# Scales and norms written as rows, weight sums at other periods, one slot without v: attention and feed-forward on one core

## Chip, cores and metric

One core of a Trainium2 chip runs the whole program. The metric is the device time of one execution in microseconds, the median of several executions. TensorE (PE), VectorE (DVE), ScalarE (ACT), GpSimd (POOL) and SyncE (SP) each run their own instructions in order; SP and POOL issue the DMAs here, and a DMA that waits for something holds up what is queued behind it on its issuing engine.

## What is computed

The reference, cut to what matters (B = 4, N = 6080, C = 256, d_ff = 2048, 24320 tokens):

```python
qn = q / (norm(q, axis=1) + 1e-6)
kn = k / (norm(k, axis=1) + 1e-6)
s = kn.transpose(0, 2, 1) @ qn / tau          # C x C scores of each batch
a = exp(s - s.max(-1)); a /= a.sum(-1) + 1e-9
x = (v @ a).reshape(B * N, C)
h = x @ w_in
g = maximum(0.01 * h, h)
out = g @ w_out
```

## The kernel before

The attention matrix of a batch is multiplied into w_in, so that v is taken straight to h; then g and the second product follow. Products are made of f16 or f32 halves: three matmuls each (high by high, low by high, high by low). There are 24 tiles of tokens (6 a batch, 512 or 496 columns twice) and 8 pairs of blocks of d_ff in each; one tile and pair is a **period**, numbered 8 x tile + pair, 192 in all. The first product of a period takes seven block products instead of eight (Strassen's way: sums of blocks are multiplied). From tile 15 to tile 22 (`FAST`, periods 120 to 183) the second product takes seven too, and needs sums of the w_out blocks.

The order of the work is written out when the program is built. Each period has slots on VectorE, ScalarE and TensorE (`slot`, line 1529 and on), each with room for some estimated microseconds. Side work stands in queues and is taken into a slot while it fits; in the slot "dve" the queue "dve_idle" comes last, after everything else. `at(w, fn)` puts work into the queues when period w begins. What an engine runs is in that order.

Buffers called `temp` (nine, `TEMPS`) hold the copies `h` of block products (ScalarE, line 1206, three a period), the output tiles `o_sb`, the squares `sq`, the units of q and k, and the four intermediate tiles of one `wo_sums` job. A buffer is free again when its last reader is through, for an output tile when its store has landed.

The places that the change touches:
- `Scale` (class, line 147 and on) finds one power of two for a tensor: maxima per partition, then the maximum over the partitions. `gather` (line 166) writes the 128 maxima as a column to DRAM from SP (line 170, `v_scale_line` and the like: 128 pieces of 4 bytes), `read` (line 190) a period later reads that line back to all partitions, into the tile `zeros`. It waits on SP until the column has landed. Tiles from 16 on use `spread` (line 174) instead, without DRAM: a copy, a transpose (lines 177, 178) and copies. The way over DRAM is taken twelve times: two weight scales, ten tiles of v.
- `inverse` (line 508) writes the 4 x 128 inverse norms of the last batch as four columns in one DMA from POOL (line 517, `n_line`), and reads them back as a row to all partitions (line 518).
- `wo_sums(m)` (line 1002), m = 0 to 3, makes the w_out sums that the seven products of pairs 2m and 2m + 1 need: two whole-tile additions (line 1012), four half-tile operations (line 1023), and for two results a ScalarE cast (line 1031) and a subtraction (line 1034), all its VectorE steps in "dve_idle". `SUMS_AT` starts jobs 0, 1, 2 at periods 79, 83, 85; job 3 starts behind the last scores product (line 1679).
- `fast_slot` (line 1369) lays out a period of tiles 15 to 22. Its first "dve" slot (line 1388) takes v work, the splitting of the next tile's v into the operands of the first product.
- In the last tile the slot "dve_out" (line 2395) takes additions of line 1327 that finish tile 22's outputs.
- Stores to `w_dram` (line 896, from POOL) write split weights that ScalarE (line 841) and VectorE (line 853) made; their buffers (three, each in two halves) are free when the store has landed.

Of the kernel before, what the change touches and what calls it, by code (L numbers as in the profile page):

```python
# [19 lines left out]
QUAD = 32  # L20
# [10 lines left out]
RBUFS = 4  # L31
RSQRT_MAGIC = float(0x5F3759DF)
TOP = 12
SUMS_AT = (79, 83, 85)
UNITS = 5
SCORES_AT = {1: (8, 20), 2: (48, 22), 3: (0, 0)}
NORMS_AT = 80
# [6 lines left out]
def channel_attention_ffn(  # L44
# [17 lines left out]
    nc = tc.nc  # L62
# [16 lines left out]
    NPAIR = NF // 2  # L79
# [20 lines left out]
    zeros = const.tile([P, P], F32, name="zeros")  # L100
# [3 lines left out]
    ones_r = const.tile([P, P], F32R, name="ones")  # L104
    nc.vector.tensor_scalar(out=ones_r, in0=zeros, scalar1=1.0, scalar2=None, op0=ALU.add)
    ones = ones_r.bitcast(F32)
    exp_bias = const.tile([P, 1], F32, name="exp_bias")
    nc.vector.memset(exp_bias, -896.0 * 2.0**23)
    tau_t = const.tile([P, 1], F32, name="tau_t")
# [37 lines left out]
    class Scale:  # L147
# [18 lines left out]
        def gather(self):  # L166
            last = nc.vector.tensor_reduce(out=self.top, in_=self.most, axis=AX.X, op=ALU.max)
            if self.near:
                return self.spread()
            nc.sync.dma_start(out=self.line, in_=self.top)  # L170
            at(now[0] + 1, self.read)
            return last

# [75 lines left out]
    class Scores:  # L249
# [258 lines left out]
        def inverse(self):  # L508
            t, n = self.nt, 2 * CH
            nc.vector.tensor_tensor(out=t, in0=self.nx, in1=self.ny, op=ALU.mult)  # L510
            nc.vector.tensor_scalar(out=t, in0=t, scalar1=1e-6, scalar2=2.0**-TOP, op0=ALU.add, op1=ALU.mult)
            rn = small.tile([P, n], F32, name="rn")
            last = nc.vector.reciprocal(out=rn, in_=t)
            rows = spare_part(7, 8)
            self.rows = rows.rearrange("p (x c) -> p x c", x=2)
            line = dram.tile([2 * CH, P], F32, name=f"n_line{self.b}")
            nc.gpsimd.dma_start(out=line[0:n, :].rearrange("x p -> p x"), in_=rn[:, 0:n])
            nc.gpsimd.dma_start(out=rows, in_=line[0:n, :].rearrange("x p -> (x p)").partition_broadcast(P))
            at(now[0] + 2, self.start)
            return last  # L520
# [709 lines left out]
    def p_has(g):  # L1230
        return g // NPAIR in FAST
# [137 lines left out]
    def fast_slot(i, p):  # L1369

        g = i * NPAIR + p
        n = widths[i % NT]
        seeded = not (p == 0 and widths[i % NT] > widths[(i - 1) % NT])
        w_split.pop((i, p - 1) if p else (i - 1, NPAIR - 1), None)
        sums_start(g)
        order = ("P5", "P7", "P6", "P1", "P3") if p == 3 else ("P5", "P7", "P1", "P3", "P6")
        fast_outs(g, *order[:4 if p == 4 else 5])
        x, z = bank("x"), bank("z")
        block_product(i, p, x, A11, "B11", True, False)
        if seeded:  # L1380
            run("act", lambda: nc.scalar.copy(out=z[:, 0:n], in_=x[:, 0:n]))
        else:
            h11 = taken(i, x)
        if g - 1 in fast_h:
            run("act", unit, i - (p == 0), (p - 1) % NPAIR, "C12", fast_h.pop(g - 1), True)
        out(6)
        fast_do("act", high, g - 4, "T4")
        slot("dve", 3.0 if not p_has(g - 2) else 1.5)
        block_product(i, p, z, A12, "B21", not seeded, True)
        block_product(i, p, x, S2, "T2", False, False)  # L1390
        if not seeded:
            add(i, h11, z)
        run("act", unit, i, p, "C11", z if seeded else h11)
        h12 = taken(i, x)
        out(4)
        slot("dve_end", 1.5)
        fast_do("act", high, g - 1, "C12")
        run("act", high, i, p, "C11")
        fast_do("act", high, g - 2, "T1")
        fast_do("dve", low, g - 1, "C12")  # L1400
        run("dve", low, i, p, "C11")
        fast_outs(g, "P2", *(["P6"] if p == 4 else []))
        block_product(i, p, z, S1, "T1", True, False)
        block_product(i, p, x, S3, "T3", False, False)
        h22 = taken(i, x)
        add(i, h22, z)
        out(6)
        fast_do("act", high, g - 2, "T3")
        fast_do("act", high, g - 3, "T2")
        slot("act_end", 0.65)  # L1410
        if i == FAST[0]:
            slot("act", 1.4)
        fast_do("dve", low, g - 2, "T1")
        if p == 4:
            slot("dve_end", 0.8)
        fast_do("dve", low, g - 2, "T3")
        if not p_has(g - 2):
            slot("dve", 1.5)
        block_product(i, p, x, A22, "T4", False, True)
        block_product(i, p, z, S4, "B22", False, True)  # L1420
        run("act", unit, i, p, "C21", x, True)
        run("act", unit, i, p, "C22", h22)
        run("act", high, i, p, "C22")
        add(i, h12, z)
        fast_h[g] = h12
        last_outs(g)
        out(15 if p == 3 else 24)
        wide = p in (3, 4) or not p_has(g - 3)
        if not p_has(g - 3):
            run("dve", low, i, p, "C22")  # L1430
        fast_do("dve", low, g - 3, "T2")
        fast_do("dve", low, g - 4, "T4")
        slot("dve_end", 1.5)
        if p_has(g - 3):
            run("dve", low, i, p, "C22")
        if p == 4:
            slot("dve_out", 1.5)
        if p not in (0, 7) or not p_has(g - 3):
            slot("dve", 1.9 if wide else 1.45)
        if i == FAST[0]:  # L1440
            slot("dve_idle", 1.4)
            slot("act", 1.4)
# [215 lines left out]
    def unit_one(sc, j):  # L1658
        unit_ahead.append(j)
        unit_temps.append(j)  # L1660
        t = []
# [8 lines left out]
        def product():  # L1670
            unit_ahead.pop(0)
            unit_go(sc)
            splits.close(sc.at[j])
            if j == 0:
                sc.begin(None, bank("s"))
            mm = sc.product(j)
            if j == NCHUNK - 1:
                norm_work(sc)
                put_steps(wo_sums(NPAIR // 2 - 1), False, True)
            return mm  # L1680

        def low():
# [329 lines left out]
    def put_steps(steps, first, on=True):  # L2012

        def entry(n):
            then = [entry(n + 1)] if n + 1 < len(steps) else ()
            if steps[n][0] == "call":
                return ("call", lambda: (steps[n][1](*steps[n][2:]), *(put(*x) for x in then)))
            return (*steps[n], then, first or n > 0 and on)

        put(*entry(0))  # L2020
# [101 lines left out]
        at(24 + n, lambda n=n: put_steps(wo_half(n), False, False))  # L2122
    for n in range(wo_n):
        at((T16 - 1) * NPAIR + n // 2 * 2 + 3, wo_load, n)
    for m in range(NPAIR // 2 - 1):
        at(SUMS_AT[m], lambda m=m: put_steps(wo_sums(m), False, True))


# [185 lines left out]
    last = None  # L2314
    held = []
    for i in range(NTILES):
        for p in range(NPAIR):
# [15 lines left out]
            x, y, z = bank("x"), bank("z" if i else "y"), bank("z")  # L2333
# [6 lines left out]
            if last is not None:  # L2340
                leaky(i, p - 1, "C12", last)
                last = None
# [47 lines left out]
            else:  # L2390
                last = h12
            out(24)
            if i == NTILES - 1:
                slot("dve_end", 1.5)
                slot("dve_out", 1.5)
            last_outs(now[0])
            if i == NTILES - 1 and p < 4:
                outs.append(ffn_out(i, p, False))
# [37 lines left out]
```

## Time and profile before

| | us |
|---|---|
| median of 3 runs | 2085.36 |
| lowest, highest | 2080.54, 2089.03 |
| the profiled execution | 2087.1 |
| its span, first to last instruction | 2085.3 |
| TensorE busy | 2042.4 |
| VectorE, ScalarE, POOL busy | 1720.5, 1547.6, 340.1 |
| mean granted TensorE clock | 0.995 |

How to read it: all views are of the one profiled execution, in microseconds from its first instruction. PEld is TensorE's weight load, which runs beside its matmuls. A row of the windows view holds a stretch, its length, then the busy time (with the number of instructions) of PE, PEld, DVE, ACT and POOL in it, the granted TensorE clock as a share of full speed, the busy share of the 16 DMA engines and GB/s. In a timeline row the bracket at the end is the idle time of the engine just before and what ended it. A period is taken to begin with its first block product's first matmul: period 58 is 705.3 to 718.9, 89 is 1042.4 to 1066.8, 105 is 1234.1 to 1249.5, 113 is 1325.8 to 1344.0.

### The profile page before, as it was taken

What the parts mean: (1) busy time and instruction counts of PE and PEld (TensorE: products, weight loads), DVE (VectorE), ACT (ScalarE), POOL (GpSimd) and SP (SyncE); (2) the same over time, 40 slices, a digit from 0 to 9 for tenths busy, and PEclk for the clock granted to TensorE, in tenths of its full rate; (3) what the DMA queues carried; (4) which work ended last, traced back from release to release, by engine and by line L of the source; (5) the groups of instructions that cost most, each with busy time, mean ns of one, the idle gap of its engine ahead of it and who ended that gap; (6) DMA issues with size and microseconds to landing.
All of it is one profiled execution on the core that took longest, in us unless ns stands there. A gap on an engine that the chain in (4) does not pass through costs nothing.

```text
span 2085.3 us, 28200 instructions
## 1 busy us (share of the span) xinstructions
PE 2042.4 (98%) x9540; PEld 1185.9 (57%) x9540; DVE 1720.5 (83%) x3143; ACT 1547.6 (74%) x2849; POOL 340.1 (16%) x427
## 2 busy tenths in 40 slices
PE   9999999999999999999979999999999999999999
PEld 8888888888865455544435545444444444444444
DVE  8988888878788788888868878788989888888973
ACT  6577777766578788877756666678988888898874
POOL 0000000000012232120110000004433333343310
PEclk9999999999999999999989999999999999999999
DMA  9945676555576898663543332238998876777630
GB/s 365 395 164 206 202 244 214 178 171 181 184 211 183 226 251 223 188 167 99 162 117 127 107 125 75 102 120 194 198 203 195 176 151 139 141 147 143 134 70 27
DMA packets 158401, 359.84 MB, mean 173 GB/s; under 512 B 19536, under 2 KB 47696, under 8 KB 158256
## 3 DMA queue, kind: packets, MB, share of 16 engines
q1 hardware_dynamic: 104912, 251.52, 36.5%
q0 software_dynamic: 52976, 106.20, 25.8%
q8 instruction: 75, 1.23, 0.2%
q14 instruction: 70, 0.57, 0.1%
q10 hardware_dynamic: 368, 0.32, 0.0%
HBM read 221.77 MB, written 57.42 MB: 134 GB/s over the span
## 4 chain that ended last, share of the span: by engine, by line
PE 85%; DVE 5%; DMA 5%; ACT 3%; issue 1%; POOL 0%; SPq 0%; DVEq 0%; ACTq 0%; POOLq 0%
PE ps_o L1487 30%; PE ps_x L1163 21%; PE ps_z L1163 15%; PE ps_o L1300 7%; PE ps_s L385 4%; PE ps_o L385 2%; PE ps_y L1300 1%; PE ps_s L1300 1%; DVE g_pair L1261 1%; DMA g_a<-g_a 1%; DVE h L1200 1%; PE ps_s L1842 1%; DMA spare<-sq 1%; DMA g_a<-g_b 1%; DMA w_dram<-w_first 1%
## 5 line engine op out<-in xcount | busy, mean ns | idle before, releaser
L1487 PE MATMUL ps_o<-g_split,w_out_split 128*128 128x512 f16 (+3 forms) x2880 | 712.6, 383 | 0.2 <-ACT o_sb L1506 0.2
L1163 PE MATMUL ps_x<-v_split,w_split 128*128 128x512 f16 (+3 forms) x2280 | 621.1, 381 | 26.9 <-ACT h L1206 23.5
L1163 PEld LDWEIGHTS <-w_split 128*128 128x128 f16 x3024 | 293.5, 98 | 385.5 <-issue 54.6
L1200 DVE TENSOR_TENSOR h<-ps_z,h 128x512 f32<-128x512 f32 (+1 forms) x505 | 344.4, 682 | 183.3 <-ACT h L1206 160.5
L1163 PE MATMUL ps_z<-v_split,w_split 128*128 128x512 f16 (+3 forms) x1704 | 462.8, 380 | 9.3 <-DVE h L1200 9.0
L1206 ACT COPY h<-ps_x 128x512 f32<-128x512 f32 (+1 forms) x513 | 295.2, 575 | 190.0 <-PE ps_x L1163 170.2
L1193 DVE TENSOR_TENSOR g_split<-g,g_split 128x512 f16<-128x512 f32 (+3 forms) x480 | 328.6, 685 | 78.4 <-ACT g_split L1183 73.6
L1183 ACT ACTIVATE g<-h 128x512 f32<-128x512 f32 (+1 forms) x384 | 240.0, 625 | 167.9 <-DVE h L1200 165.3
L1487 PEld LDWEIGHTS <-w_out_split 128*128 128x128 f16 x1920 | 188.7, 98 | 226.1 <-issue 5.7
L1487 PEld LDWEIGHTS ps_o<-g_split,w_out_split 128*128 128x128 f32 x1152 | 216.4, 188 | 43.5
L1183 ACT ACTIVATE g_split<-h 128x512 f16<-128x512 f32 (+3 forms) x360 | 220.2, 612 | 0.0
L1261 DVE TENSOR_TENSOR g_pair<-g_b,g_pair 128x512 f16<-128x512 f32 (+1 forms) x192 | 125.1, 679 | 42.0 <-ACT g_pair L1256 41.6
L1300 PE MATMUL ps_o<-g_pair,w_out_split 128*128 128x512 f16 (+1 forms) x576 | 158.0, 377 | 0.4 <-ACT g_pair L1256 0.3
L1300 PEld LDWEIGHTS <-spare 128*128 128x128 f16 x768 | 75.1, 98 | 88.9 <-issue 0.4
L1163 PEld LDWEIGHTS ps_x<-v_split,w_split 128*128 128x128 f32 x576 | 107.8, 188 | 22.3 <-ACT g L1183 0.4
L1256 ACT CAST g_pair<-g_b 128x512 f16<-128x512 f32 (+1 forms) x192 | 111.0, 611 | 0.0
L1109 DVE SCALAR_TENSOR_TENSOR v_split<-v_raw,v_scale,v_split 128x512 f16<-128x512 f32 (+1 forms) x125 | 93.0, 744 | 3.8
L1300 PEld LDWEIGHTS <-w_out_split 128*128 128x128 f16 x576 | 56.3, 98 | 67.0 <-issue 0.6
L273 POOL MEMSET qk_raw<- 64x512 f32 x5 | 3.0, 592 | 538.1 <-ACT sq L299 267.6
L1261 DVE TENSOR_TENSOR g_pair<-g_a,g_pair 128x512 f16<-128x512 f32 (+1 forms) x128 | 86.5, 676 | 1.9 <-ACT g_pair L1256 1.5
L1183 ACT ACTIVATE g<-ps_x 128x512 f32<-128x512 f32 (+1 forms) x128 | 75.3, 588 | 15.5 <-PE ps_x L1163 13.4
L1163 PEld LDWEIGHTS ps_z<-v_split,w_split 128*128 128x128 f32 x408 | 76.2, 188 | 16.6 <-DVE h L1200 1.4
(266 smaller groups left out, 2724.5 us busy)
## 6 DMA issues: line engine op xcount, KB each, us to landing
w_split<-w_dram SPq DMA_DIRECT2D x104, 448.0 KB, 4.0
w_split<-w_dram SPq DMA_DIRECT2D x40, 896.0 KB, 5.1
qk_raw<-in_q_dram SPq DMA_DIRECT2D x115, 256.0 KB, 5.0
qk_raw<-in_k_dram SPq DMA_DIRECT2D x115, 256.0 KB, 5.1
v_raw<-in_vT_dram SPq DMA_DIRECT2D x32, 512.0 KB, 6.0
out_dram<-o_sb SPq DMA_DIRECT2D x64, 256.0 KB, 3.4
spare<-sq POOLq DMA_DIRECT2D x47, 256.0 KB, 6.1
g_a<-g_a POOLq DMA_DIRECT2D x40, 256.0 KB, 3.9
```

The source lines that it names most:

```text
L385: mm = nc.tensor.matmul(out=out, lhsT=lhsT, rhs=rhs, start=start, stop=stop, skip_group_check=True)
L1109: return nc.vector.scalar_tensor_tensor(out=sp[:, 1, 0:w], in0=src, scalar=up, in1=sp[:, 0, 0:w], op0=ALU.mult, op1=ALU.subtract)
L1163: mm = nc.tensor.matmul(out=ps[:, 0:n], lhsT=w[:, x, a, :], rhs=sp[:, y, 0:n], start=first and k == 0, stop=k == 2, skip_group_check=True,)
L1183: return nc.scalar.activation(out=to, in_=h[:, 0:n], func=AF.Prelu, alpha=0.01, scale=G_SCALE if i >= T16 else 1.0)
L1193: issued["dve"] = nc.vector.tensor_tensor(out=sp[:, 1, 0:n], in0=out[:, 0:n], in1=f32(sp[:, 0, 0:n]), op=ALU.subtract)
L1200: issued["dve"] = nc.vector.tensor_tensor(out=h[:, 0:n], in0=ps[:, 0:n], in1=h[:, 0:n], op=ALU.add)
L1206: issued["act"] = nc.scalar.copy(out=h[:, 0:n], in_=ps[:, 0:n])
L1256: return nc.scalar.copy(out=sp[:, 0, 0:n], in_=g32[i, p, HELD.get(name, name)][:, 0:n])
L1261: return nc.vector.tensor_tensor(out=sp[:, 1, 0:n], in0=g32[i, p, HELD.get(name, name)][:, 0:n], in1=sp[:, 0, 0:n], op=ALU.subtract)
L1300: issued["pe"] = nc.tensor.matmul(out=ps[:, 0:n], lhsT=fast_lhsT(i, p, prod, x), rhs=sp[:, y, 0:n], start=p == 0 and k == 0, stop=p == NPA ...
L1487: issued["pe"] = nc.tensor.matmul(out=o_ps[i][j][h][:, 0:n], lhsT=wo_lhsT(i, x, f, h), rhs=sp[:, y, 0:n], start=p == 0 and early and k == ...
L1842: last = nc.tensor.matmul(out=ps, lhsT=m[:, x, W_OF[n] * P:(W_OF[n] + 1) * P], rhs=r[:, y, :], start=n in W_OPENS and k == 0, stop=k == 2, ...
```

## The change

Scales and norms go to DRAM as rows: a new helper `turned` copies the columns into 32 columns of `zeros`, transposes 32 by 32 blocks on VectorE, and gives one view of 4 partitions x 32 for each column; line 170's DMA then has 4 pieces of 128 bytes, and line 517's DMA becomes four such DMAs. `SUMS_AT` becomes 79, 113, 121, 122 and starts all four jobs; the start of job 3 behind the last scores product goes. The first "dve" slot of a seven-product period has room 0 in pair 4, where it had 1.5, once such periods are under way. The last tile's "dve_out" slot has room for 0.8 us instead of 1.5. The arithmetic is the same.

```diff
--- before.py
+++ after.py
@@ -31,7 +31,7 @@
 RBUFS = 4
 RSQRT_MAGIC = float(0x5F3759DF)
 TOP = 12
-SUMS_AT = (79, 83, 85)
+SUMS_AT = (79, 113, 121, 122)
 UNITS = 5
 SCORES_AT = {1: (8, 20), 2: (48, 22), 3: (0, 0)}
 NORMS_AT = 80
@@ -104,6 +104,14 @@
     ones_r = const.tile([P, P], F32R, name="ones")
     nc.vector.tensor_scalar(out=ones_r, in0=zeros, scalar1=1.0, scalar2=None, op0=ALU.add)
     ones = ones_r.bitcast(F32)
+
+    def turned(columns, n, at=0):
+
+        a, b = zeros[:, at:at + QUAD], zeros[:, at + QUAD:at + 2 * QUAD]
+        nc.vector.tensor_copy(out=a[:, 0:n], in_=columns)
+        last = nc.vector.transpose(out=b, in_=a)
+        return last, [b.rearrange("(q r) c -> q r c", r=QUAD)[:, x, :] for x in range(n)]
+
     exp_bias = const.tile([P, 1], F32, name="exp_bias")
     nc.vector.memset(exp_bias, -896.0 * 2.0**23)
     tau_t = const.tile([P, 1], F32, name="tau_t")
@@ -167,7 +175,8 @@
             last = nc.vector.tensor_reduce(out=self.top, in_=self.most, axis=AX.X, op=ALU.max)
             if self.near:
                 return self.spread()
-            nc.sync.dma_start(out=self.line, in_=self.top)
+            last, rows = turned(self.top, 1)
+            nc.sync.dma_start(out=self.line.rearrange("(q c) o -> q (o c)", c=QUAD), in_=rows[0])
             at(now[0] + 1, self.read)
             return last
 
@@ -510,11 +519,13 @@
             nc.vector.tensor_tensor(out=t, in0=self.nx, in1=self.ny, op=ALU.mult)
             nc.vector.tensor_scalar(out=t, in0=t, scalar1=1e-6, scalar2=2.0**-TOP, op0=ALU.add, op1=ALU.mult)
             rn = small.tile([P, n], F32, name="rn")
-            last = nc.vector.reciprocal(out=rn, in_=t)
+            nc.vector.reciprocal(out=rn, in_=t)
+            last, turned_rn = turned(rn, n, 2 * QUAD)
             rows = spare_part(7, 8)
             self.rows = rows.rearrange("p (x c) -> p x c", x=2)
             line = dram.tile([2 * CH, P], F32, name=f"n_line{self.b}")
-            nc.gpsimd.dma_start(out=line[0:n, :].rearrange("x p -> p x"), in_=rn[:, 0:n])
+            for x, row in enumerate(turned_rn):
+                nc.gpsimd.dma_start(out=line[x].rearrange("(q c) -> q c", c=QUAD), in_=row)
             nc.gpsimd.dma_start(out=rows, in_=line[0:n, :].rearrange("x p -> (x p)").partition_broadcast(P))
             at(now[0] + 2, self.start)
             return last
@@ -1385,7 +1396,7 @@
             run("act", unit, i - (p == 0), (p - 1) % NPAIR, "C12", fast_h.pop(g - 1), True)
         out(6)
         fast_do("act", high, g - 4, "T4")
-        slot("dve", 3.0 if not p_has(g - 2) else 1.5)
+        slot("dve", 3.0 if not p_has(g - 2) else 1.5 if p != 4 else 0.0)
         block_product(i, p, z, A12, "B21", not seeded, True)
         block_product(i, p, x, S2, "T2", False, False)
         if not seeded:
@@ -1676,7 +1687,6 @@
             mm = sc.product(j)
             if j == NCHUNK - 1:
                 norm_work(sc)
-                put_steps(wo_sums(NPAIR // 2 - 1), False, True)
             return mm
 
         def low():
@@ -2122,7 +2132,7 @@
         at(24 + n, lambda n=n: put_steps(wo_half(n), False, False))
     for n in range(wo_n):
         at((T16 - 1) * NPAIR + n // 2 * 2 + 3, wo_load, n)
-    for m in range(NPAIR // 2 - 1):
+    for m in range(NPAIR // 2):
         at(SUMS_AT[m], lambda m=m: put_steps(wo_sums(m), False, True))
 
 
@@ -2392,7 +2402,7 @@
             out(24)
             if i == NTILES - 1:
                 slot("dve_end", 1.5)
-                slot("dve_out", 1.5)
+                slot("dve_out", 0.8)
             last_outs(now[0])
             if i == NTILES - 1 and p < 4:
                 outs.append(ffn_out(i, p, False))
```

## Rows read from the trace of the kernel before

**Rows 1.** The page, part 1: busy time (share of the span) xinstructions, by engine.
```profile
PE 2042.4 (98%) x9540; PEld 1185.9 (57%) x9540; DVE 1720.5 (83%) x3143; ACT 1547.6 (74%) x2849; POOL 340.1 (16%) x427
```

**Rows 2.** Waits of TensorE: in total us, times, longest us.
```profile
PE ps_x L1163 <- ACT h L1206: 23.5, 9, 11.7
PE ps_z L1163 <- DVE h L1200: 9.0, 20, 1.0
```

**Rows 3.** Windows of periods 58, 89, 90, 105 and 113.
```profile
705.30:718.90 13.60, 10.52 (x50) 5.07 (x49) 8.58 (x15) 8.96 (x17) 4.32 (x6) 1.00 0.89 158
1042.40:1066.80 24.40, 12.27 (x46) 4.99 (x45) 11.51 (x24) 10.47 (x25) 3.17 (x5) 0.73 0.60 86
1066.80:1076.60 9.80, 9.80 (x47) 4.46 (x46) 6.84 (x15) 5.13 (x10) 2.73 (x4) 0.99 0.41 158
1234.10:1249.50 15.40, 13.14 (x58) 5.96 (x57) 10.74 (x19) 8.55 (x17) 0.00 (x0) 0.89 0.38 131
1325.80:1344.00 18.20, 13.16 (x53) 5.39 (x52) 8.89 (x16) 8.66 (x17) 0.00 (x0) 0.91 0.33 117
```

**Rows 4.** Timeline of ScalarE, period 89: start us, us, instruction, [idle before].
```profile
1060.80 0.61 ACT L841 ACTIVATE w_first<-w_c 128x128 f16<-128x128 f32 x2 [11.98 <-DMA w_dram<-w_first]
```

**Rows 5.** Timeline of POOL, periods 88 and 89.
```profile
1042.11 0.85 POOL L517 DMA_DIRECT2D n_line<-rn  x1
1045.36 0.67 POOL L896 DMA_DIRECT2D w_dram<-w_first  x1 [2.39 <-ACT h L1206]
```

**Rows 6.** DMA issues, 1040 to 1062 us: count, KB each, median us to landing.
```profile
w_dram<-w_first POOLq DMA_DIRECT2D x1, 256.0 KB, 15.4
...
n_line<-rn POOLq DMA_DIRECT2D x1, 2.0 KB, 11.5
...
v_scale_line<-v_scale SPq DMA_DIRECT2D x1, 0.5 KB, 11.6
```

**Rows 7.** DMA issues, 1000 to 1040 us.
```profile
w_dram<-w_first POOLq DMA_DIRECT2D x3, 256.0 KB, 2.4
```

**Rows 8.** Source view of line 170, the twelve scale columns.
```profile
DMA to landing us min/median/max: 7.1/7.8/11.7
```

**Rows 9.** Tile view of the output stores, `out_dram`.
```profile
DMA to landing us min/median/max: 1.9/3.4/14.3
```

**Rows 10.** Timeline of ScalarE, period 58.
```profile
713.35 0.58 ACT L1206 COPY h<-ps_x 128x512 f32<-128x512 f32 x1 [3.58 <-DMA spare<-sq]
```

**Rows 11.** Timelines of SP, ScalarE and VectorE, period 113.
```profile
1329.01 0.32 SPq L190 DMA_DIRECT2D zeros<-v_scale_line  x1
...
1336.02 0.58 ACT L1206 COPY h<-ps_x 128x512 f32<-128x512 f32 x1 [5.47 <-DMA out_dram<-o_sb]
...
1335.32 0.42 DVE L1023 TENSOR_TENSOR wo_s<-wo_a 128x256 f32<-128x256 f32 x1 [4.05 <-DMA out_dram<-o_sb]
```

**Rows 12.** Timeline of ScalarE, period 105.
```profile
1239.77 0.58 ACT L1206 COPY h<-ps_x 128x512 f32<-128x512 f32 x1 [3.41 <-DMA out_dram<-o_sb]
```

**Rows 13.** Timeline of VectorE: first and last step of a `wo_sums` job.
```profile
985.42 0.68 DVE L1012 TENSOR_TENSOR wo_a<-w_out_split 128x512 f32<-128x512 f16 x1
...
1293.26 0.69 DVE L1034 TENSOR_TENSOR spare<-wo_s,spare 128x512 f16<-128x512 f32 x1
```

**Rows 14.** Source view of line 1023: duration ns min/median/max, first and last start.
```profile
L1023 DVE TENSOR_TENSOR wo_s<-wo_a x8: 411/418/425, 951.1 to 1335.3; 128x256 f32<-128x256 f32 x8
```

**Rows 15.** Windows of periods 114 to 117 and 121 to 124.
```profile
1344.00:1390.60 46.60, 46.60 (x218) 21.14 (x217) 36.71 (x71) 32.26 (x65) 2.02 (x3) 1.00 0.33 99
1419.70:1452.10 32.40, 30.87 (x136) 13.12 (x135) 26.74 (x60) 27.92 (x54) 14.36 (x17) 1.00 0.88 206
```

**Rows 16.** Windows of pairs 4 and 7 of tile 16.
```profile
1514.60:1525.10 10.50, 10.50 (x51) 4.89 (x50) 7.53 (x14) 7.53 (x14) 3.35 (x4) 1.00 0.87 168
1541.50:1549.60 8.10, 8.10 (x40) 3.78 (x39) 6.11 (x11) 7.42 (x15) 1.78 (x3) 1.00 0.98 219
```

**Rows 17.** Timeline of VectorE, last tile, pair 4.
```profile
2030.64 1.26 DVE L1327 TENSOR_TENSOR o_sb<-o_sb 128x496 f32<-128x496 f32 x2
```

## The prediction

> **What bounds the kernel now.** I read the busy totals first, then who TensorE waits for, then TensorE's idle time period by period, then the engine behind each large gap. In [rows 1] the reader sees TensorE busy 2042.4 of 2085.3 us, so no edit that leaves the matmuls alone can win more than about 43 us, plus what a lowered clock costs. [rows 2] say where that idle time is: 23.5 us in nine waits for the copy `h` (line 1206, ScalarE), 11.7 us of them in one wait, and only 9.0 us in twenty waits for the addition at line 1200 (VectorE), none over 1.0 us. So a few long waits are worth more than all the short ones. [rows 3] place four of the long ones (a period is numbered 8 x tile + pair; a stretch's idle time is its length less its PE busy time):
> - period 58: 13.60 - 10.52 = 3.1 us idle, clock at 1.00: **3.1 us**.
> - period 89: 24.4 us, where the next period with about the same number of matmuls (47 against 46) takes 9.8 us: **14.6 us**, 12.1 of it idle. The granted clock is 0.73 over the stretch, so part of it ran at 1.2 GHz instead of 2.4.
> - period 105: 15.40 - 13.14 = 2.3 us idle, and a clock of 0.89 over 15.4 us is 1.7 us of lost work: **4.0 us**.
> - period 113: 18.20 - 13.16 = 5.0 us idle, and 9% of 18.2 is 1.6 us: **6.7 us**.
> Together 28.4 us.
>
> **What stands behind them.** Period 89: ScalarE sat 11.98 us before line 841 until a store `w_dram<-w_first` had landed [rows 4]; it needed that store's buffer. The store was issued at 1045.36 [rows 5] and took 15.4 us to land, beside `n_line<-rn`, 2 KB in 11.5 us, and `v_scale_line`, 0.5 KB in 11.6 us [rows 6]. Shortly before, the same stores took 2.4 us [rows 7]. So two column writes of a few bytes per piece hold everything that is in flight with them. A column write of a scale takes at least 7.1 us, whatever is beside it [rows 8], a full store of 256 KB as little as 1.9 [rows 9]. Period 58: ScalarE waited 3.58 us for a transfer out of a `temp` buffer, `spare<-sq` [rows 10], while the longest of the twelve `v_scale_line` and like columns, 11.7 us [rows 8], was out. Period 113: line 190, the read of that column, issues at 1329.01 when the column has landed; the stores `out_dram<-o_sb` stand behind it on SP's queue; ScalarE (5.47 us) and VectorE (4.05 us) wait for their `temp` buffers [rows 11]. Period 105: ScalarE waits 3.41 us for the same kind of buffer [rows 12], but no column is out then. There the pool is short for another reason: a job of `wo_sums` that started at 985.42 was still writing its last result at 1293.26 [rows 13], because "dve_idle" is served last; for 300 us it kept some of the nine `temp` buffers.
>
> **The change part by part.**
> **Rows instead of columns.** Twelve scale columns (128 pieces of 4 bytes) become rows of 4 pieces of 128 bytes; the norms' column (512 pieces) becomes four DMAs of 4 pieces. No row of the trace shows a write of a few 128-byte pieces. Its bounds are a full store's 1.9 us [rows 9] and the column's 7.1 us [rows 8]. I take about 2 us: the column's 0.5 KB is far less data than the store's 256 KB, so what takes 7 us must be the number of pieces, and that falls from 128 to 4. Then the store of 1045.36 lands as before in 2.4 us, or in 5 if the queues are full: between 1047.8 and 1050.4, where line 841 wants it at 1048.8 (1060.80 less 11.98, [rows 4]); 0 to 1.6 us of wait may remain, I take 0. Period 58's transfer lands before it is wanted. In period 113, SP goes on 7.1 - 2 = 5.1 us earlier, just over the 5.0 us idle. All three gaps go: 3.1 + 14.6 + 6.7 = 24.4 us. What is added: per write a copy of one column and a transpose of 32 columns on VectorE, each under the 0.42 us of an operation on 256 columns [rows 14]; 13 times 0.8 is at most 11 us spread over 1000 us, on an engine with idle time around each place: nothing, and if it all stood in TensorE's way, 11 us. POOL issues four DMAs instead of one, at the 0.85 us of the old one [rows 5] 2.6 us more, ahead of the store of 1045.36: it may leave 0.3 us late. New waits: the copy writes into `zeros`, which the scale before (some eight periods earlier) was read from and sent from, so it finds it free; line 170 waits for two short operations more, and the stores behind it on SP with it, less than 0.8 us. What is late next in period 89 is TensorE itself: the following period is wholly busy [rows 3].
> What the row shows is that a small write is slow, not yet why. The Trainium skill, "DMA: Bandwidth & Descriptors", section Specifications, speaks against the change: below 512 B a DMA does a read-modify-write. A piece of 128 bytes is still below. If that alone made the column slow, the row would be no quicker; this is the second rival.
>
> **The sums moved.** Jobs 1 and 2 no longer start at periods 83 and 85 and lie about; jobs 1, 2, 3 start at 113, 121, 122. Period 105's shortage goes (two or more buffers come free): 4.0 us. A job is four whole-tile VectorE operations of 0.68 us [rows 13], four half-tile ones of 0.42 [rows 14], so 4.4 us, and two ScalarE casts; it issues no DMA, so no queue of SP or POOL changes by the move. Job 1 falls into 1344 to 1391, where VectorE has 46.6 - 36.7 = 9.9 us idle [rows 15]: hidden. If that cover were gone it would cost its 4.4. Jobs 2 and 3, 8.8 us, fall into 1420 to 1452, the first seven-product periods, where VectorE has 32.4 - 26.7 = 5.7 us idle [rows 15]. 8.8 - 5.7 = **3.1 us lost**. Bounds: 0 (TensorE has 1.5 us of idle in that stretch too, and a job can run on into the next periods) and 8.8.
>
> **No v in front in pair 4.** In eight tiles up to 1.5 us of VectorE's v work in front of pair 4 moves to later slots. In such a period TensorE is busy all 10.50 us, and VectorE has 3.0 us idle [rows 16]: nothing to win. The two subtractions of 1.4 us or so go to the last pairs, where VectorE has 8.1 - 6.1 = 2.0 us idle [rows 16]: nothing lost. If that cover is gone, 1.4 x 8 = 11 us lost at most; a gain is excluded, since TensorE doesn't idle there. I take 0.
> **The last tile.** At most one addition of line 1327 per period instead of two; the pair took 1.26 us in front of line 1200 [rows 17], and half of it, **0.6 us**, comes off one of the twenty short waits; at most 1.0 [rows 2], at least 0.
>
> **The sum**, made against the profiled execution's own 2087.1 us (span 2085.3, 1.8 us around it): 2087.1 - 24.4 - 4.0 - 0.6 + 3.1 = **2061 us**. The median of the runs shown is 1.7 us lower and they spread over 8.5 us, so the sum has about that much play besides.
>
> **The rivals.**
> *Half the gain.* Rows are quick, but periods 105 and 113 stay short of `temp` buffers: in 113 job 1 now holds up to four of nine where job 3 held them, beside four stores. For it: the same place, the same number. Against it: the stores leave 5 us earlier. Then only 58 and 89 are won: 2087.1 - 17.7 - 0.6 + 3.1 = 2072.
> *Rows as slow as columns.* The write is slow because its pieces are small, not because they are many. For it: the norms' write has four times the scale's pieces and took 11.5 us against 11.6 [rows 6], not four times as long. Against it: the 256 KB stores with large pieces, and that those two disturbed each other. Then 58, 89 and 113 stay: 2087.1 - 4.0 - 0.6 + 3.1 = 2086. By the 512 B rule of the Trainium skill ("DMA: Bandwidth & Descriptors", Specifications) it would be this.
> *Slower.* From period 121 jobs 2 and 3 run interleaved and hold up to eight of nine `temp` buffers, while ScalarE needs three per period for `h`. Each period then stalls like 113 did, 6.7 us. It outweighs the 29.0 us won when it lasts more than 4.3 periods; over 121 to 125 it is 33.5: 2087.1 - 29.0 + 33.5 = 2092. For it: [rows 13], a job can lie about for hundreds of us. Against it: first-tile slots of the seven-product code give "dve_idle" 1.4 us of its own.
>
> **How the numbers follow.** Forecast (2061) 0.78, half the gain 0.09, slow rows 0.08, slower 0.05. Low end: the jobs free (3.1), the last tile 1.0 instead of 0.6, the median's 1.7 lower and some 3 us of play: 2061 - 8 = 2053. High end: the forecast with the jobs at 8.8 is 2067, half the gain with some play 2075; beyond lie 0.13 of the chances. About 0.5% (10.4 us, so 2075 and 2096 as seen from 2085.4) is what a measurement of this kernel tells from no change. Faster: the first two, less 0.01 for play: 0.86. Same: slow rows and that 0.01: 0.09. Slower: 0.05, the last rival counted on its far side.
>
> **What would show it.** In the profile after: `v_scale_line` lands in 2 to 3 us and `n_line` in under 4; no ScalarE wait over 2 us before line 841 in period 89, which lasts about 10 us; lines 190 and 1514 follow at once in period 113; no `temp` wait at 105; four `wo_sums` jobs that each finish within four periods, and 1 to 5 us more in periods 121 to 125; pair 4 of the seven-product tiles unchanged. Rows that land in 7 us, or new `temp` waits after 1420, would make the prediction wrong.

## The result, and the profile after

| | before | after |
|---|---|---|
| median of the runs | 2085.51 us | 2062.62 us |
| lowest, highest | 2080.54, 2089.03 | 2061.71, 2063.18 |
| span of the profiled execution | 2085.3 | 2060.9 |
| TensorE busy | 2042.4 | 2037.4 |
| mean granted TensorE clock | 0.995 | 1.0 |

The ratio of after to before is 0.9892, 95% interval 0.9871 to 0.9912. The forecast was 2061 us, the range 2053 to 2075.

Line numbers after the change are 11 higher than before in most of the file (1163 is 1174, 1200 is 1211, 1206 is 1217, 170 is 179, 190 is 199, 841 is 852, 1012 is 1023, 1023 is 1034, 1031 is 1042, 1034 is 1045).

TensorE's waits after, in total us, times and longest (against [rows 2]):

```profile
PE ps_z L1174 <- DVE h L1211: 8.7, 21, 1.1
PE ps_x L1174 <- ACT h L1217: 2.7, 5, 0.7
PE ps_x L1174 <- ACT g_a L1255: 2.2, 2, 1.2
PE ps_z L1174 <- ACT ps_z L1392: 1.8, 2, 1.6
...
PE ps_o L1311 <- DVE g_pair L1272: 1.0, 1, 1.0
```

The wait for the copy `h` on ScalarE fell from 23.5 us with a longest of 11.7 to 2.7 with a longest of 0.7. The many short waits on VectorE's addition are as they were. Two rows are new: a wait of 1.6 us for a copy into `ps_z`, and one of 1.0 for `g_pair`. They come back below.

The windows of periods 58, 89, 90, 105, 113, 121 and 122 after (stretch, length, then busy us of PE, PEld, DVE, ACT, POOL, granted clock, DMA share, GB/s; against [rows 3]):

```profile
705.60:716.10 10.50, 10.50 (x50) 5.08 (x49) 8.87 (x15) 9.15 (x18) 4.31 (x6) 1.00 0.86 210
1039.60:1049.90 10.30, 9.86 (x47) 4.40 (x46) 10.13 (x23) 8.59 (x21) 4.42 (x8) 1.00 0.51 165
1049.90:1060.40 10.50, 9.80 (x47) 4.37 (x46) 8.46 (x19) 6.77 (x15) 3.06 (x5) 1.00 0.55 185
1217.90:1229.70 11.80, 11.80 (x64) 6.17 (x63) 11.05 (x21) 7.95 (x15) 0.00 (x0) 1.00 0.54 180
1305.40:1317.10 11.70, 11.70 (x56) 5.32 (x55) 9.89 (x18) 8.22 (x16) 0.00 (x0) 1.00 0.58 179
1393.20:1401.40 8.20, 6.95 (x31) 2.90 (x30) 7.77 (x28) 5.91 (x13) 2.49 (x3) 1.00 0.76 237
1401.40:1411.50 10.10, 7.66 (x32) 2.92 (x31) 7.46 (x14) 7.02 (x14) 4.16 (x5) 1.00 0.91 192
```

The first column less the PE column is the idle time. It is 0 in 58, 105 and 113, and the granted clock is 1.00 in 89, 105 and 113, where it was 0.73, 0.89 and 0.91. Taken by period (from the first matmul of one to that of the next), in us before and after:

| period | before | after | difference | forecast |
|---|---|---|---|---|
| 58 | 13.65 | 10.46 | -3.19 | -3.1 |
| 89 and 90 | 24.43 + 9.74 | 10.28 + 10.51 | -13.4 | -14.6 |
| 105 to 110 together | | | -4.2 | -4.0 |
| 113 | 18.16 | 11.65 | -6.51 | -6.7 |
| 121, 122 | 7.16, 8.85 | 8.20, 10.07 | +2.26 | +3.1 with the next row |
| 114 to 120 and 123 to 127 | | | +0.42 + 0.52 | |
| 188 (last tile, pair 4) | 14.29 | 13.70 | -0.59 | -0.6 |

105 is taken with its neighbours because products moved between these periods. These sum to -24.7; the whole difference in span is -24.4. What is left lies in periods 55 (+0.4), 128 (-0.4), 143 (+1.1) and 144 (-0.9), which vary by as much from kernel to kernel here (55: 10.4 to 12.4 us; 143: 8.2 to 9.4).

Period 89 closely. POOL, then ScalarE (before: [rows 4, 5]), then the DMA issues from 1036 to 1056 us (count, KB each, median us to landing; before: [rows 6]):

```profile
1039.42 2.22 POOL L528 DMA_DIRECT2D n_line<-zeros  x4
1042.71 0.74 POOL L907 DMA_DIRECT2D w_dram<-w_first  x1 [1.07 <-ACT h L1217]
1044.85 0.58 POOL L529 DMA_DIRECT2D spare<-n_line  x1 [1.40 <-DMA n_line<-zeros]
```
```profile
1045.99 0.60 ACT L852 ACTIVATE w_first<-w_c 128x128 f16<-128x128 f32 x2
1049.92 0.72 ACT L852 ACTIVATE w_first<-w_s 128x256 f16<-128x256 f32 x2
```
```profile
w_dram<-w_first POOLq DMA_DIRECT2D x3, 256.0 KB, 2.6
...
n_line<-zeros POOLq DMA_DIRECT2D x4, 0.5 KB, 3.4
```

The four row writes of the norms land in 3.4 us, where the column took 11.5; the stores of the same size as the one that took 15.4 us take 2.6; line 852 runs without a bracket, that is without a wait, where line 841 waited 11.98 us.

The scale's way over DRAM in period 105 after (VectorE's two new operations, the write, and its read):

```profile
1225.29 0.15 DVE L111 COPY zeros<-v_scale 128x1 f32<-128x1 f32 x1
...
1225.47 0.21 DVE L112 STREAM_TRANSPOSE zeros<-zeros 128x32 f32<-128x32 f32 x1
...
1225.71 0.50 SPq L179 DMA_DIRECT2D v_scale_line<-zeros  x1
...
1227.26 0.33 SPq L199 DMA_DIRECT2D zeros<-v_scale_line  x1
```

The profile gives no landing for the row write. Line 199 waits on SP for it and issues 1227.26 - 1225.71 = 1.55 us behind it, so it had landed by then; the column took at least 7.1 [rows 8]. Over all twelve scales the read follows the write by 1.55 to 2.3 us in nine cases and by 3.3, 3.7 and 5.7 in three; the 5.7 is the scale just before period 58, where the column took 11.7. The two added VectorE operations take 0.15 + 0.21 us.

### The profile page after: what moved, and what is told of

Its sections match the earlier page's. It is cut to its first block, busy times and chain, and to the rows that moved or that the text cites. A ratio compares the mean times of both kernels' runs of the same rounds, so it can differ in the third digit from the quotient of the medians.

```text
span 2060.9 us, 28218 instructions
## 1 busy us (share of the span) xinstructions
PE 2037.4 (99%) x9540; PEld 1184.7 (57%) x9540; DVE 1726.7 (84%) x3169; ACT 1546.9 (75%) x2849; POOL 336.0 (16%) x430
## 4 chain that ended last, share of the span: by engine, by line
PE 86%; DVE 7%; ACT 3%; DMA 2%; issue 1%; POOL 0%; SPq 0%; DVEq 0%; ACTq 0%; POOLq 0%
PE ps_o L1498 30%; PE ps_x L1174 21%; PE ps_z L1174 16%; PE ps_o L1311 7%; PE ps_s L394 4%; PE ps_o L394 2%; PE ps_y L1311 1%; PE ps_s L1311 1%; DVE g_pair L1272 1%; DVE h L1211 1%; PE ps_s L1852 1%; PE ps_y L394 1%; DMA g_a<-g_b 1%; ACT h L1217 1%; DMA spare<-sq 1%
## 5 line engine op out<-in xcount | busy, mean ns | idle before, releaser
L1194 ACT ACTIVATE g<-ps_x 128x512 f32<-128x512 f32 (+1 forms) x128 | 75.4, 589 | 14.6 <-PE ps_x L1174 12.5
```

Of the source, the lines that this page charges most:

```text
L1194: return nc.scalar.activation(out=to, in_=h[:, 0:n], func=AF.Prelu, alpha=0.01, scale=G_SCALE if i >= T16 else 1.0)
```

## The experiments

Each ratio is to the kernel before, run on the same chip, with its 95% interval; the kernel before had medians of 2083.0 to 2090.0 us there. All compute the whole of the reference.

**The two halves of the change.** rows_only is the kernel before with the rows of lines 170 and 517 alone (the first, second and third part of the diff with `turned`); sums_only is the kernel before with the moved sums alone:

```diff
-SUMS_AT = (79, 83, 85)
+SUMS_AT = (79, 113, 121, 122)
-                put_steps(wo_sums(NPAIR // 2 - 1), False, True)
-    for m in range(NPAIR // 2 - 1):
+    for m in range(NPAIR // 2):
```

> The kernel before with the rows alone (scales and norms); the sums and the slots stay as they were. Theory (columns block the transfers in flight and SP's queue): the gaps of periods 58, 89 and 113 go (3.1 + 14.6 + 6.7 = 24.4 us off 2085.5), the gap of 105 stays, nothing is lost at 121: 2061 us, the same as the changed kernel. Rival (period 113 is short of temp buffers whatever the stores do): 113 stays, 17.7 off: 2068 us.

Measured: 2064.55 us in the median of four runs from 2060.24 to 2068.78, ratio 0.9872 (0.9843 to 0.9900), profiled span 2058.5. Period 58 -3.24, 89 -14.14, 113 -6.54; period 105 keeps 2.31 us of TensorE's idle time (105 to 110 together are 1.6 us shorter, the granted clock being 1.00 there instead of 0.89), and periods 114 to 127 are not lengthened (0.00).

> The kernel before with the w_out sums at 79, 113, 121, 122 alone; columns stay. Theory: only the gap of period 105 goes (4.0), periods 121 and 122 lose 2.3 to 3.1, the gaps of 58, 89 and 113 stay: 2084 to 2085 us, no difference that can be measured. Rival (the jobs' temp buffers also made the gap of 113): another 6.7 off, 2078 us.

Measured: 2087.89 us, ratio 0.9988 (0.9971 to 1.0006), span 2087.3. Periods 105 to 110 together are 4.2 us shorter; 121 is +1.04 and 122 +1.22, and 114 to 127 together +3.8; 58 (16.16 us), 89 (25.27) and 113 keep their gaps, and the first two are even longer (+2.5, +0.8).

What follows: the rows alone win all of what the change wins. The sums remove one gap and make new ones of about its size; the two cancel to nothing that can be measured. Beside the rows, which already give back 1.6 us at 105, the sums win 2.6 there and lose 3.2 in 114 to 127 (3.6 without the new slot of pair 4, see below). The places of the two effects are separate, so each half can be read in the other's absence.

**The slots.** slots_back is the changed kernel with both slots as before:

```diff
-        slot("dve", 3.0 if not p_has(g - 2) else 1.5 if p != 4 else 0.0)
+        slot("dve", 3.0 if not p_has(g - 2) else 1.5)
-                slot("dve_out", 0.8)
+                slot("dve_out", 1.5)
```

> The changed kernel with both slots back as before (1.5 in front of pair 4 of the seven-product periods, 1.5 for the last tile's additions). Theory: pair 4 is worth nothing, the last tile 0.6: 2063.2 against 2062.6 us, and pair 4 takes as long as in the changed kernel. Rival (v in front of pair 4 delays TensorE): at least 0.3 us in each of eight tiles, 2065.5 us or more.

Measured: 2063.51 us, ratio 0.9868 (0.9845 to 0.9891), span 2060.6. Period 188 is 14.29 us again, +0.59. Pair 4 is unchanged in seven of the eight tiles, but in the first, tile 15, period 124 takes 8.71 us instead of 8.41 and period 125 8.83 instead of 8.71; sums_only, which has the old slots too, shows the same 8.70 and 8.83, and with the sums at their old places (rows_only) v in front costs nothing there, 8.41. So the new slot of pair 4 is worth about 0.4 us, and only where the moved sums load VectorE. In the whole time neither part can be seen, in the periods both can.

**Which column.** norms_row makes only the norms rows, scales_row only the scales (rows_only without one of its two parts):

> The kernel before with the norms alone as rows; the twelve scales stay columns, sums and slots stay. Theory: in period 89 the store that ScalarE needs leaves at about 1045 and lands before the scale column of 1049 goes out, so the gap of 89 goes (13 to 14 us), those of 58, 105 and 113 stay: about 0.9935 of before. Rival (one column is enough to hold that store): the scale column of period 89 holds it until 1049.4 + 7.1 = 1056.5, ScalarE waits some 7 us instead of 12: about 0.997.

> The kernel before with the twelve scales alone as rows; the norms stay one column of 512 pieces. Theory: 58 and 113 go (3.2 + 6.5); in 89 the norms column still holds the store of 1045.4 until it has landed itself at about 1053.6, so ScalarE waits 5 us instead of 12: 16 to 18 us off, about 0.992 of before. Rival (the gap of 89 was the scale column's alone): all three go, 24 us off, 0.988.

Measured: norms_row 2074.08 us, 0.9952 (0.9936 to 0.9969), span 2075.2; scales_row 2072.94 us, 0.9952 (0.9937 to 0.9966), span 2071.4. Both won less than was expected (0.9935 and 0.992); by place period 89 did about as expected in both, -14.15 and -6.12 us, and the rest is spread: in norms_row 90 and 113 are 1.2 us longer each, in scales_row 145 is 1.7 longer. Period 89 in each, norms_row first, and the ScalarE wait that is left in scales_row:

```profile
1043.20:1053.40 10.20, 9.76 (x46) 4.35 (x45) 9.67 (x21) 8.49 (x21) 4.31 (x8) 1.00 0.53 165
```
```profile
1038.60:1056.90 18.30, 12.30 (x46) 4.93 (x45) 11.90 (x26) 10.50 (x25) 3.19 (x5) 0.84 0.74 113
```
```profile
1050.90 0.61 ACT L849 ACTIVATE w_first<-w_c 128x128 f16<-128x128 f32 x2 [5.84 <-DMA w_dram<-w_first]
```

What follows: the norms' column opens period 89's gap. Without it the gap is gone, although the scale's column is still there. With it and no scale column ScalarE waits 5.84 us, with both 11.98 [rows 4]. So the scale's column, issued in the midst of that wait, doubles it, and by itself does no such harm: in norms_row period 90 is 1.15 us longer than before, in the changed kernel 0.8. Periods 58 and 113 are the scales' alone: in scales_row 58 is -3.24 and 113 -6.54, in norms_row both keep their gaps.

**What makes the column slow.** Seven extra writes were put into the changed kernel, each from a `temp` buffer to a DRAM tile of its own from SP, read back by POOL, which nothing else holds up there:

```diff
+            nc.sync.dma_start(out=d[:, 0:cols], in_=t[0][0:rows, 0:cols])
+            nc.gpsimd.dma_start(out=t[0][0:1, P:P + 1], in_=d[0:1, 0:1])
```

In a first form, without the read-back (probes), the writes waited for nothing:

> The changed kernel with seven extra small writes from SP to places in DRAM that nobody reads, one in each of periods 99, 100, 101, 103, 107, 108, 109: 128 pieces of 4 B in one run of 512 B; 128 pieces of 4 B, each 512 B apart; 128 of 128 B; 128 of 512 B; 32 of 4 B; 4 of 4 B; 4 of 128 B. Theory (the number of pieces makes the time): 7, 7, 7, 7, 3, 2 and 2 us to landing. First rival (pieces below 512 B are slow by their size): all about 7 us but the fourth, which lands in 2 to 3. Second rival (pieces that fall into the same 512 B wait for each other): 7, 2 to 3, 2 to 3, 2 to 3, 3, 2, 2.

They were issued at 32 to 50 us, in the crowded start, and the first product began at 94.25 us instead of 85.45; the one run took 2070.41. No landing could be read, so it decides nothing on the shapes. The second form:

> The changed kernel with seven extra small writes from SP (sources: a temp buffer that VectorE has just filled; one in each of periods 99, 100, 101, 103, 107, 108, 109), each read back by an otherwise idle POOL queue, whose issue tells when the write has landed: 128 pieces of 4 B in one run of 512 B; 128 of 4 B, each 512 B apart; 128 of 128 B; 128 of 512 B; 32 of 4 B; 4 of 4 B; 4 of 128 B. Theory (the number of pieces makes the time): 7, 7, 7, 7, 3, 2 and 2 us. First rival (pieces below 512 B are slow by their size): all about 7 us but the fourth, 2 to 3. Second rival (pieces that fall into the same 512 B wait for each other): 7, 2 to 3, 2 to 3, 2 to 3, 3, 2, 2.

Two of the seven, SP's issue and POOL's read-back of each:

```profile
1151.82 0.33 SPq L2136 DMA_DIRECT2D probe_128x4B_run<-probe  x1
...
1160.57 0.55 POOL L2137 DMA_DIRECT2D probe<-probe_128x4B_run  x1 [102.39 <-DVE unit L347]
```
```profile
1175.44 0.32 SPq L2136 DMA_DIRECT2D probe_128x128B<-probe  x1
1177.45 0.51 POOL L2137 DMA_DIRECT2D probe<-probe_128x128B  x1 [8.22 <-DMA probe_128x128B<-probe]
```

From issue to read-back, one sample each, and from issue to the end of POOL's wait for that write, which comes 0.5 to 0.7 us before the read-back:

| pieces | where | us to read-back | us to the end of the wait |
|---|---|---|---|
| 128 of 4 bytes | in one run of 512 bytes (the old column) | 8.75 | 8.0 |
| 128 of 4 bytes | 512 bytes apart | 3.32 | 2.7 |
| 128 of 128 bytes | in one run | 2.01 | 1.4 |
| 128 of 512 bytes | in one run, beside other transfers | 4.25 | 3.7 |
| 32 of 4 bytes | in one run of 128 bytes | 3.97 | 3.5 |
| 4 of 4 bytes | in one run of 16 bytes | 1.73 | 1.1 |
| 4 of 128 bytes | in one run of 512 bytes (the new row) | 1.66 | 1.2 |

What follows: 128 pieces alone are not slow (2.01), nor are four pieces below 512 bytes (1.66), nor even 128 pieces of 4 bytes where each lies in a place of its own (3.32). Slow is the write of many 4-byte pieces into the same few hundred bytes, and it grows with their number: (8.75 - 1.73) / 124 is 0.06 us for each further piece, an estimate from two samples (it gives 3.3 for 32 pieces, where 3.97 was measured). The Trainium skill, "DMA: Bandwidth & Descriptors", section Specifications, has a read-modify-write below 512 B. A rule by which every such piece is slow doesn't agree with 128 pieces of 128 bytes in 2.01 us; that pieces which change the same 512 bytes have to wait for one another would fit the three runs of 4-byte pieces, but no run here shows it directly.

Where the time of the slow write lies, the same trace shows. The DMA view from 1152.6 to 1152.9 us, then from 1152.9 to 1159.8, and the first of POOL's waits in the source view of line 2137 (first and last start):

```profile
DMA packets 144, 0.00 MB, mean 2 GB/s; under 512 B 144, under 2 KB 144, under 8 KB 144
```
```profile
DMA packets 0, 0.00 MB, mean 0 GB/s; under 512 B 0, under 2 KB 0, under 8 KB 0
```
```profile
L2137 POOLq EVENT_SEMAPHORE  x16: 17/43/43, 1159.9 to 1267.0; - x16
```

All packets of the write (128 of 4 bytes and 16 more) are through 1.0 us after its issue; then the DMA engines show none for seven us, until the write counts as landed at 1159.9. So it isn't the handling of 128 packets that takes the time, but something behind them that no view shows: 7.0 us here, 2.4 behind the 32 pieces, 0.3 to 0.5 behind the writes of 128 x 128, 128 x 512, 4 x 4 and 4 x 128 bytes. In the kernel before, the column of period 113 is the same: 144 packets through by 1322.9, none from there to 1328.9, and its read at 1329.01 [rows 11].

When other transfers are under way, they go slowly in that time. The DMA view of the kernel before from 1046 to 1052 us, in period 89:

```profile
DMA packets 98, 0.19 MB, mean 32 GB/s; under 512 B 10, under 2 KB 90, under 8 KB 98
...
q1 hardware_dynamic: 90, 0.16, 82.0%
q0 software_dynamic: 8, 0.03, 15.4%
```

The 16 engines count as busy for 97% of this stretch and move 32 GB/s, where period 135 moved 219 GB/s at a busy share of 0.98 [rows 16]. All the probes went out from SP; the norms' column, from POOL, opens the longest gap, and no probe had its shape. That the same cause makes it slow is argued from the likeness, not shown.

**The `temp` buffers of period 105.** hold_temps takes two of the nine buffers away in periods 104 to 109 of the changed kernel (two one-column copies on VectorE, and one addition to free them); hold4 takes four. If the gap of 105 is a want of buffers and nothing else, it should come back:

```diff
+        for _ in range(2):
+            held_temps.append(temp(name="held"))
+            last = nc.vector.tensor_copy(out=held_temps[-1][:, 0:1], in_=ident[:, 0:1])
+    at(104, put, "dve", 0.2, hold_begin, (), True)
+    at(109, put, "dve", 0.1, hold_end, (), True)
```

> The changed kernel with two temp buffers taken at period 104 and given back at 109, written and read by copies of one column, so that almost no VectorE work comes with it. Theory (the gap of period 105 came from two held temp buffers): it comes back, 3.5 to 4.2 us, 2066 to 2067 us. Rival (it came from the VectorE work of the sums in those periods): it stays away, 2062.6 us.

> The changed kernel with four temp buffers (instead of the two of the earlier run) held from period 104 to 109, without VectorE work. Theory (periods 104 and 105 need more than five of the nine at once): ScalarE waits for temp buffers there and the gap of 105 is back, at least 2 us. Rival (buffers are not what 105 lacked): no gap, 2062.5 us.

Measured: hold_temps 2062.39 us, ratio 0.9861 (0.9839 to 0.9884), no gap at 105; hold4 2062.49 in its one run, span 2060.6, period 105 longer by 0.80 us with 0.32 of wait. Both miss the theory as it was put. Its converse, buffers given instead of taken, held. rows_wtmp is rows_only, with the sums at their old places, and only the two results of each job of `wo_sums` (line 1015) come from another pool of eight buffers:

```diff
-            s = t[name] = temp(name="wo_s").rearrange("p (k s c) -> p k s c", k=2, s=2)
+            s = t[name] = w_tmp("wo_s").rearrange("p (k s c) -> p k s c", k=2, s=2)
```

> The kernel before with the rows, sums left at 79, 83, 85 and the end of the scores as before, but the two results of a sums job in buffers of another pool (w_tmp) instead of temp. VectorE's order stays that of the run with rows alone. Theory (period 105 stalls because temp buffers are held): its gap of 2.7 us goes, and nothing is lost at 121 and 122, so about 2.5 us less than the changed kernel: 2060 us where that has 2062.6. Rival (the sums' VectorE work in period 104 delays what frees the buffers): the gap stays, 2062 to 2064 us.

Measured: 2060.23 us, ratio 0.9859 (0.9838 to 0.9880), span 2058.3. Period 105 in rows_only and ScalarE's wait in it, then the same in rows_wtmp:

```profile
1216.80:1230.50 13.70, 11.39 (x58) 5.53 (x57) 10.61 (x21) 8.28 (x15) 0.00 (x0) 1.00 0.43 149
```
```profile
1222.46 0.59 ACT L1216 COPY h<-ps_x 128x512 f32<-128x512 f32 x1 [3.46 <-DMA out_dram<-o_sb]
```
```profile
1217.90:1229.40 11.50, 11.20 (x59) 5.56 (x58) 11.06 (x21) 8.49 (x17) 0.00 (x0) 1.00 0.53 183
```
```profile
1220.08 0.58 ACT L1216 COPY h<-ps_x 128x512 f32<-128x512 f32 x1
```

What follows: with the same order of VectorE's work (in both kernels two operations of line 345 stand ahead of the output tiles) and the same stores behind the q and k loads, two buffers more take the wait away. So in that order it is the buffers. In the changed kernel only one such operation stands ahead of the output tiles and a store leaves SP ahead of the q and k loads (at 1219.33, the loads at 1219.76), and there even four buffers fewer cost 0.80 us. The gap of 105 needed both: the held buffers and the order; the change removed both at once. Which part of the order counts, VectorE's operation or SP's store, no run separates.

**The price of the moved sums.** sums_117 is the changed kernel with jobs 2 and 3 earlier, where the prediction's counting found VectorE with more idle time:

```diff
-SUMS_AT = (79, 113, 121, 122)
+SUMS_AT = (79, 113, 117, 121)
```

> The changed kernel with the sums at 79, 113, 117, 121 instead of 79, 113, 121, 122, so that only one job is left for the first seven-product periods. Theory (those periods lose VectorE time to two jobs): 1 to 2.5 us off 2062.6, periods 121 and 122 shorter by about half of the 2.3 us that they gained. Rival (job 2 finds no room in 117 to 120 and only moves the loss there): the same 2062.6.

Measured: 2065.44 us, ratio 0.9914 (0.9899 to 0.9929), span 2063.6: worse than the changed kernel's span by 2.7, where a gain was expected. Period 121 is 9.05 us (8.20 in the changed kernel) and 122 is 12.97 (10.07). The job's whole-tile operations ran in period 119, but its half-tile ones only in 121, at 1394.9 to 1398.5, and job 3 right behind them.

Why these periods pay is in the changed kernel's own rows: VectorE, then ScalarE, then TensorE, in periods 121 and 122:

```profile
1398.22 0.68 DVE L1023 TENSOR_TENSOR wo_a<-w_out_split 128x512 f32<-128x512 f16 x1
1398.82 1.28 DVE L1272 TENSOR_TENSOR g_pair<-g_b,g_pair 128x512 f16<-128x512 f32 x2
...
1403.02 0.68 DVE L1023 TENSOR_TENSOR wo_a<-w_out_split 128x512 f32<-128x512 f16 x1
1403.74 0.42 DVE L1034 TENSOR_TENSOR wo_s<-wo_a 128x256 f32<-128x256 f32 x1
1404.20 0.43 DVE L1034 TENSOR_TENSOR wo_s<-wo_s,wo_a 128x256 f32<-128x256 f32 x1
```
```profile
1404.66 0.62 ACT L1042 CAST spare<-wo_s 128x512 f16<-128x512 f32 x1 [2.28 <-DVE wo_s L1034]
1405.18 0.58 ACT L1392 COPY ps_z<-ps_x 128x512 f32<-128x512 f32 x1
```
```profile
1399.55 0.38 PE L1311 MATMUL ps_o<-g_pair,w_out_split 128*128 128x512 f16 x1 [1.03 <-DVE g_pair L1272]
...
1405.81 0.81 PE L1174 MATMUL ps_z<-v_split,w_split 128*128 128x512 f16 x3 [1.63 <-ACT ps_z L1392]
```

In 121 an addition of the sums runs in front of `g_pair`, and TensorE waits 1.03 us for that. In 122 it is ScalarE: the job's cast, line 1042, stands in its queue ahead of the copy into `ps_z`, waits 2.28 us for the sums on VectorE, and TensorE waits 1.63 us for the copy. In rows_wtmp, where no job lies here, that copy (line 1391 there) runs at 1401.78 without a wait, and the two periods take 7.16 and 8.57 us. The two waits, 1.03 + 1.63 us, are about the 2.3 that the periods grew by. sums_only has the same two waits (1.0 and 1.6 us), so they come with the sums; that the cast is the step that counts in 122 is read from the rows, and no run moved it alone.

**The best of both.** rows_wtmp with the last tile's slot of the change:

```diff
-                slot("dve_out", 1.5)
+                slot("dve_out", 0.8)
```

> Scales and norms as rows, the sums' and pairs' places as in the kernel before, the 128x512 results of line 170 that wait for the second products' weights in the second pool instead of the temps, and the last tile's last part on VectorE by a share that begins earlier (0.8). Theory (the gap of period 105 is a want of temp buffers, and later jobs of sums cost what they displace): period 105 at 11.5 us, periods 121 and 122 at 7.2 and 8.6, the end 0 to 0.6 us sooner; about 0.985 to 0.987 of the kernel before, 1 to 3 us under the changed kernel. Rival (what the later sums cost is paid elsewhere when they stay early): the same as the changed kernel, 0.989.

(The line meant there as 170 is 1015.) Measured: 2059.72 us, ratio 0.9870 (0.9853 to 0.9886), span 2058.3. Period 105 takes 11.48 us, 121 and 122 take 7.16 and 8.61, and 188 is -0.58. Its profiled span is 2.6 us under the changed kernel's, and by the periods 2.5 of that are 121 and 122. The two ratios, 0.9870 and 0.9892, overlap in their intervals, and the two kernels were not timed side by side; the gain is shown by place, not by the total.

## Why the prediction was right

- **The rows, -24.4 us.** Right in place and size: -3.19, -14.15 and -6.51 in periods 58, 89 and 113, 23.9 together, less 0.8 that period 90 is longer; rows_only has the same three without the rest of the change. The value taken for a row write, about 2 us, was 1.55 to 2.3 for nine of the twelve scales, 3.3 to 5.7 for the others, and 3.1 to 3.8 for the norms; the store behind the norms landed in 2.5 us all the same. The step "1.9 to 7.1, nearer the store" was the one on which the forecast hung.
- **Its reason was only half right.** "What takes 7 us must be the number of pieces" falls: 128 pieces of 128 bytes took 2.01 us. For a scale's column it is many 4-byte pieces in the same few hundred bytes. The rival that small pieces are slow as such fell too. The change would have been right by any reason that makes 4 pieces of 128 bytes quick; that the wrong reason did no harm was luck.
- **The sums, -4.0 in 105.** The size was right (-4.2), though 1.6 of it comes with the rows, by the clock. "The pool is short" was right for the order of the kernel before (rows_wtmp) and not enough for the order of the kernel after (hold_temps, hold4): the change moved the order too, which the prediction didn't look at.
- **The sums, +3.1.** The size was right (3.2 in periods 114 to 127, 2.3 of it in 121 and 122), the reckoning was not, so the agreement is luck. It set VectorE's work against VectorE's idle time over four periods. What cost time was where the steps stand in the order of two engines, and over half of it was ScalarE, whose casts were counted in the prediction and given no price (by the rows, the 1.2 us that period 122 grew). sums_117, reckoned by the same idle time, went the other way.
- **Pair 4 at nothing, the last tile -0.6.** Period 188 gave 0.59, as forecast. Pair 4 at nothing was right in seven tiles; "a gain is excluded" was read from tile 16 and doesn't hold in tile 15, where the moved sums run and the slot saves 0.4 us (slots_back). The loss of 3.2 us above is what is left after that.
- **The rivals.** Half the gain: period 113 has no wait left, though job 1 now lies in it from 1308 to 1326 us. Slower: job 3 lasted from 1415 to 1449 us, five periods, but the copy `h` made TensorE wait 0.7 us at most.
- **What was expected of the profile** and came otherwise: the row of a scale took 1.6 to 5.7 us instead of 2 to 3, and job 3 longer than four periods. POOL's four issues for the norms took 2.22 us together, 1.4 more than the one before, where 2.6 more was reckoned.

## What to carry to other kernels

A few bytes per partition that go to DRAM should be turned into a row on chip first: two operations of 0.36 us together and a row write, mostly of 1.6 to 2.3 us, took the place of a write of 7 to 12 us, and the larger gain was that the stores beside it landed in 2.6 us instead of 15.4. When work is moved to a stage with idle time, look at what stands right behind each of its steps on each in-order engine, the small cast on the second engine too; an engine's idle sum over the stage doesn't tell it. When a pool runs short, giving one user another pool (rows_wtmp) can be cheaper than moving that user to another time.

## What was not expected of the hardware

Writes of 0.5 and 2 KB in 4-byte pieces don't only land late themselves: beside the norms' column a store of 256 KB took 9.3 us (scales_row), beside both columns 15.4, where 2.4 was usual [rows 6, 7], and the two together about doubled ScalarE's wait (5.84 and 11.98 us). The lateness isn't the DMA engines' work: the packets of a lone column were through after 1.0 us, and it landed 6 to 7 us later. The same 128 pieces of 4 bytes spread 512 bytes apart took 3.32 us instead of 8.75. After the longest gaps were gone the granted clock stayed at 1.00 through all of these periods, and 5.0 us of the 24.4 won are TensorE's busy time (2042.4 to 2037.4) at the same number of matmuls.
